# Token-major local attention and on-chip casts of the first two batches in a fused attention and MoE kernel

## The chip, the cores and the metric

The kernel runs on one core of a Trainium2 chip. The metric is the device time of one execution in microseconds (us). Before the change it is 374.99 us, the median of three runs (374.14 to 375.85).

A ratio is the mean time of one kernel's fast runs over the mean time of the other's fast runs of the same rounds, so it is not quite the ratio of the medians that are quoted beside it. The profile is of one execution, and its span is about 1.7 us shorter than the time of that execution.

## The reference

There are 8 batches, 8 heads of 64 columns, 512 local tokens and 32 global tokens per batch. Local queries see the keys at most 32 positions away and all global keys. Global queries see everything. A mixture-of-experts layer with a single expert (no routing) follows.

```
k_all, v_all = cat([k_g, k_l]), cat([v_g, v_l])
out_g = softmax(scale * q_g @ k_all.T) @ v_all
s_ll  = where(abs(pos_i - pos_j) <= 32, scale * q_l @ k_l.T, -1e9)
out_l = softmax(cat([scale * q_l @ k_g.T, s_ll])) @ v_all
x     = cat([out_g, out_l])            # (8 * 544) tokens x 512
h     = x @ w_in                       # 512 -> 2048
out   = (h * clip(h + 3, 0, 6) / 6) @ w_out
```

All inputs are fp32 in DRAM. The kernel computes in fp16, so every input is cast once.

## The kernel before

The work goes in 32 turns, one per pair of heads, four turns per batch. Turn p transposes the keys and queries of pair p + 2, computes the scores of pair p + 1 and the values of pair p, and fills the gaps with units of the previous batch's MoE (`M(n)` takes n units; one unit is four 512-column matmuls). A batch has 32 units.

```python
# loads: Pool's software queue casts fp32 to fp16 on the way in, one head at a time for batch 0
def load_head(b, h):
    qn, kn = nat[b]
    for t, src in ((kn, k_l), (qn, q_l)):
        nc.gpsimd.dma_start(out=t[:, :, h], in_=src[b, h].rearrange("(kb p) d -> p kb d", p=P))
# ... order at the start: k, q of batch 0, v of batch 0, then
load_qk(1, False); load_v(1)                 # batch 1
for m in range(NM): nc.gpsimd.dma_start(out=w_in_t[m], ...)     # 4 x 512 KB as fp16
for c4 in range(NC // 4): nc.gpsimd.dma_start(out=w_out_t[c4], ...)

# values: stationary = values, moving = exp of the scores; output is feature-major
nc.tensor.matmul(out=pav[:, 0:Sl], lhsT=vgz[:, b, h], rhs=EG[:, 0:Sl], ...)
for kb in range(NT):
    nc.tensor.matmul(out=pav[:, lo:lo + w], lhsT=vn[b % NV][:, kb, h], rhs=E[...], ...)
nc.scalar.activation(out=Ln, in_=pav[D:P, 0:Sl], func=LN)       # 1/sum = exp(-ln(sum))
nc.scalar.activation(out=Rc, in_=Ln, func=EXP, scale=-1.0)
nc.vector.tensor_tensor(out=xts[b][m][r], in0=Rc[r], in1=pavs[e][0:D, 0:Sl], op=mult)

for p in range(NPAIR):                       # cut to its order
    emit_T(p + 2); M(1); emit_QK(p + 1); M(2); emit_G(...); M(2); emit_AV(p, lambda: M(1)); M(2)
```

The softmax here doesn't subtract the row's maximum and nothing guards it: scores larger than these inputs give would overflow.

Of the kernel before, what the change touches and what calls it, by code (L numbers as in the profile page):

```python
# [14 lines left out]
def kernel(  # L15
# [12 lines left out]
    nc = tc.nc  # L28
# [6 lines left out]
    NQ = NM // 2  # L35
# [3 lines left out]
    WB = P + 2 * W  # L39
    HALF = 2 * WB - W  # L40
    EW = HALF + 2 * Sg
# [10 lines left out]

    WIN = []
    for kb in range(NT):
        lo = max(kb * P - W, 0)
        hi = min(kb * P + P + W, Sl)
        WIN.append((lo, hi - lo))
    COL = [0, WIN[0][1], 0, WIN[2][1]]
    assert WIN[0][1] + WIN[1][1] == HALF and WIN[2][1] + WIN[3][1] == HALF

    constp = ctx.enter_context(tc.tile_pool(name="constp", bufs=1))
    natp = ctx.enter_context(tc.tile_pool(name="natp", bufs=2))
    wrk = ctx.enter_context(tc.tile_pool(name="wrk", bufs=2))
    moew = ctx.enter_context(tc.tile_pool(name="moew", bufs=4))
# [6 lines left out]
    nc.scalar.preload_act_table_set("natural_log_exp_and_others")  # L71

    def const(name, shape, dtype=FP16):
        return constp.tile(shape, dtype, tag=name, name=name)

    ident = const("ident", [P, P])
    kgz = const("kgz", [P, B, NM, P])
    vgz = const("vgz", [P, B, H, P])
    qgT = const("qgT", [P, NM, B, Sg])
    half_col = const("half_col", [P, 1], FP32)  # L80
    mask = [const(f"mask{i}", [P, HALF]) for i in range(2)]
    NV = 3
    vn = [const(f"vn{i}", [P, NT, H, P]) for i in range(NV)]
    w_in_t = [const(f"win{m}", [P, dff]) for m in range(NM)]
    w_out_t = [const(f"wout{c}", [P, 4, dm]) for c in range(NC // 4)]

    nat = {}

    def load_qk(b, by_head):
        kn = natp.tile([P, NT, H, D], FP16, tag="kn", name="kn")  # L90
        qn = natp.tile([P, NT, H, D], FP16, tag="qn", name="qn")
        nat[b] = (qn, kn)
        if not by_head:
            for t, src in ((kn, k_l), (qn, q_l)):
                for kb in range(NT):
                    nc.gpsimd.dma_start(  # L96
                        out=t[:, kb],
                        in_=src[b, :, kb * P:(kb + 1) * P, :].rearrange("h s d -> s h d"))

    def load_head(b, h):  # L100
        qn, kn = nat[b]
        for t, src in ((kn, k_l), (qn, q_l)):
            nc.gpsimd.dma_start(out=t[:, :, h],  # L103
                                in_=src[b, h].rearrange("(kb p) d -> p kb d", p=P))

    def load_v_head(b, h):
        nc.gpsimd.dma_start(out=vn[b % NV][:, :, h, 0:D],  # L107
                            in_=v_l[b, h].rearrange("(kb p) d -> p kb d", p=P))

    def load_v(b):  # L110
        for kb in range(NT):
            nc.gpsimd.dma_start(  # L112
                out=vn[b % NV][:, kb, :, 0:D],
                in_=v_l[b, :, kb * P:(kb + 1) * P, :].rearrange("h s d -> s h d"))

    make_identity(nc, ident)
    load_qk(0, True)
    for h in range(4):
        load_head(0, h)

    gnat = []
    for src, nm in ((k_g, "kg"), (q_g, "qg")):
        t = const(nm + "n", [P, 2, H, D], FP32)
        for g in range(2):
            for b4 in range(4):
                nc.sync.dma_start(out=t[b4 * Sg:(b4 + 1) * Sg, g],
                                  in_=src[g * 4 + b4].rearrange("h s d -> s h d"))
        gnat.append(t)


    base = const("mbase", [P, WB])
    nc.vector.memset(base, 1.0)
    nc.gpsimd.affine_select(out=base, in_=base, compare_op=is_ge, fill=0.0,
                            base=0, pattern=[[1, WB]], channel_multiplier=-1)
    nc.gpsimd.affine_select(out=base, in_=base, compare_op=is_ge, fill=0.0,
                            base=2 * W, pattern=[[-1, WB]], channel_multiplier=1)
    nc.vector.tensor_copy(out=mask[0][:, 0:WB - W], in_=base[:, W:WB])
    nc.vector.tensor_copy(out=mask[0][:, WB - W:HALF], in_=base)
    nc.vector.tensor_copy(out=mask[1][:, 0:WB], in_=base)
    nc.vector.tensor_copy(out=mask[1][:, WB:HALF], in_=base[:, 0:WB - W])  # L140

    for h in range(2):
        load_v_head(0, h)
    load_head(0, 4)
    load_head(0, 5)

    nc.vector.memset(half_col, 0.5)
    for i in range(NV):
        nc.vector.memset(vn[i][:, :, :, D:P], 1.0)
    nc.vector.memset(kgz, 0.0)  # L150
    nc.vector.memset(vgz, 0.0)

    def pos(h):
        return (h % 2) * 2 + (h // 2) % 2

    for i in range(4):
        h0 = [h for h in range(4) if pos(h) == i][0]
        r = slice(i * Sg, (i + 1) * Sg)
        for qd in range(NQ):
            nc.vector.memset(vgz[r, :, 4 * qd + h0, D:P], 1.0)  # L160
            nc.gpsimd.dma_start(out=vgz[r, :, 4 * qd + h0, 0:D],  # L161
                                in_=v_g[:, 4 * qd + h0].rearrange("b s d -> s b d"))

    load_v_head(0, 2)
    load_v_head(0, 3)
    load_head(0, 6)
    load_head(0, 7)
    for h in range(4, 8):
        load_v_head(0, h)
    load_qk(1, False)  # L170
    load_v(1)
    for m in range(NM):
        nc.gpsimd.dma_start(out=w_in_t[m], in_=moe_w_in[m * P:(m + 1) * P, :])
    for c4 in range(NC // 4):
        nc.gpsimd.dma_start(
            out=w_out_t[c4],
            in_=moe_w_out[c4 * 4 * P:(c4 + 1) * 4 * P, :].rearrange("(c p) n -> p c n", p=P))


    gnat16 = []  # L180
    for t, nm in zip(gnat, ("kg", "qg")):
        t16 = const(nm + "n16", [P, 2, H * D])
        nc.vector.tensor_copy(out=t16, in_=t.rearrange("p g h d -> p g (h d)"))  # L183
        gnat16.append(t16)

    def emit_globals(g):
        psT = ps_tile("psGT", FP16)
        for w in range(2):
            for m in range(NM):
                nc.tensor.matmul(out=psT[:, (w * NM + m) * P:(w * NM + m + 1) * P],  # L190
                                 lhsT=gnat16[w][:, g, m * P:(m + 1) * P],
                                 rhs=ident, is_transpose=True)
        kv = psT.rearrange("p (w q pp b s) -> p w q pp b s", w=2, q=NQ, pp=2, b=4)
        for pp in range(2):
            for e in range(2):
                c0 = (e * 2 + pp) * Sg
                for qd in range(NQ):
                    nc.scalar.copy(
                        out=kgz[e * D:(e + 1) * D, g * 4:(g + 1) * 4, 2 * qd + pp, c0:c0 + Sg],
                        in_=kv[e * D:(e + 1) * D, 0, qd, pp])  # L200
        nc.vector.tensor_copy(
            out=qgT[:, :, g * 4:(g + 1) * 4],
            in_=psT[:, NM * P:2 * NM * P].rearrange("p (m b s) -> p m b s", m=NM, b=4))

    st = {}

    def emit_T(p):
        b, m = divmod(p, NM)
        qn, kn = nat[b]
        psT = ps_tile("psT", FP16)  # L210
        for w, t in enumerate((kn, qn)):
            for j in range(NT):
                nc.tensor.matmul(out=psT[:, w * Sl + j * P:w * Sl + (j + 1) * P],  # L213
                                 lhsT=t[:, j, 2 * m:2 * m + 2].rearrange("p h d -> p (h d)"),
                                 rhs=ident, is_transpose=True)
        kT = wrk.tile([P, Sl], FP16, tag="kT", name="kT", bufs=4)
        qT = wrk.tile([P, Sl], FP16, tag="qT", name="qT", bufs=4)
        nc.vector.tensor_copy(out=kT, in_=psT[:, 0:Sl])  # L218
        nc.scalar.copy(out=qT, in_=psT[:, Sl:2 * Sl])  # L219
        st[p] = dict(qT=qT, kT=kT)  # L220

    def emit_QK(p):
        b, m = divmod(p, NM)
        s = st[p]
        qT, kT = s["qT"], s["kT"]
        E = wrk.tile([P, 2, 2, EW], FP16, tag="E", name="E", bufs=3)
        s["E"] = E
        for half in range(2):
            pss = [ps_tile(f"psS{e}") for e in range(2)]
            for kb in (2 * half, 2 * half + 1):  # L230
                lo, w = WIN[kb]
                for e in range(2):
                    nc.tensor.matmul(out=pss[e][:, COL[kb]:COL[kb] + w],  # L233
                                     lhsT=kT[e * D:(e + 1) * D, kb * P:(kb + 1) * P],
                                     rhs=qT[e * D:(e + 1) * D, lo:lo + w])
                g0 = HALF + (kb % 2) * Sg
                for e in range(2):
                    nc.tensor.matmul(out=pss[e][:, g0:g0 + Sg],  # L238
                                     lhsT=kT[e * D:(e + 1) * D, kb * P:(kb + 1) * P],
                                     rhs=qgT[e * D:(e + 1) * D, m, b])  # L240
# [27 lines left out]
    def emit_AV(p, mid):  # L268
# [11 lines left out]
        for e in range(2):  # L280
# [18 lines left out]
            if e == 0:  # L299
                mid()  # L300
# [60 lines left out]
    for p in range(NPAIR):  # L361
# [4 lines left out]
        if p == 1:  # L366
            emit_globals(1)
# [52 lines left out]
```

## Time and profile before

These lines are from the page of the kernel before. They are the busy times, the rows of TensorE (PE), Pool, transfers (DMA) and moved data over 40 equal slices of 9.4 us, the two DMA queues that matter (packets, MB as written, share of 16 engines), and the chain of waits by engine.

```profile
PE 332.3 (89%) x2608; PEld 178.9 (48%) x2608; DVE 235.6 (63%) x489; ACT 239.5 (64%) x473; POOL 102.6 (27%) x132
...
PE   0078589999999999999999999999999999999995
...
POOL 8999436923240307003700343000000000000000
...
DMA  9999999999390469119961949100001000100202
GB/s 131 120 77 141 199 204 169 152 131 84 44 101 29 75 67 110 32 58 86 68 47 56 114 27 86 50 36 30 2 30 56 30 2 28 58 28 0 87 29 56
...
q0 software_dynamic: 104896, 17.05, 60.7%
q1 hardware_dynamic: 9344, 9.97, 7.9%
...
PE 62%; DVE 12%; POOL 9%; ACT 9%; issue 3%; DMA 3%; POOLq 0%
```

From the sixth slice on TensorE is busy at eight tenths or more. Until then it is not, and in that time the transfers are at nine tenths or more: for the first ten slices, to 94 us, their row has no gap. The chain of waits in order of time shows what the start hangs on. Columns are start, length, and what ran.

```profile
1.34 0.89 POOL kn L103
...
20.32 0.97 POOL kn L96
...
31.99 3.49 POOL vn_82 L112 x4
35.48 0.55 POOL win_84 L173
...
36.44 11.94 DMA win_86<-in_moe_w_in_dram
48.43 0.61 PE psH L324
```

Pool issues the casting loads one after the other until 36 us, and the first MoE matmuls then wait for `w_in`. I read off two points from the timeline of TensorE: the transposes that open a turn (`psT<-ident,kn`), and the first MoE matmul (`psH`), which stands right behind the opening of turn 4, the first turn of batch 1.

### The profile page before, as it was taken

How to read it: one execution, taken by the hardware profiler on the slowest of the kernel's cores; microseconds unless marked ns; L12 is line 12 of the kernel's file. 1: busy time of each engine (PE TensorE's matmuls, PEld its weight loads, DVE VectorE, ACT ScalarE, POOL GpSimd, SP SyncE). 2: the span in 40 equal slices, each digit the busy share in tenths (PEclk: the TensorE clock that was granted, in tenths of full speed). 3: DMA queues.
4: the chain of work that ended last, by engine and by line, in shares of the span. 5: the costliest groups of instructions: out<-in, count | busy, mean ns of one | idle time of the engine just before them, and what ended most of it. 6: DMA issues, size and time to landing. Idle time of an engine off the chain costs nothing.

```text
span 375.0 us, 6707 instructions
## 1 busy us (share of the span) xinstructions
PE 332.3 (89%) x2608; PEld 178.9 (48%) x2608; DVE 235.6 (63%) x489; ACT 239.5 (64%) x473; POOL 102.6 (27%) x132
## 2 busy tenths in 40 slices
PE   0078589999999999999999999999999999999995
PEld 0046335555455554554555445545555445544472
DVE  7855667645875487548764587448754885296171
ACT  1059969745984599547965698458945895375070
POOL 8999436923240307003700343000000000000000
PEclk9998969999999999999999999999999999999999
DMA  9999999999390469119961949100001000100202
GB/s 131 120 77 141 199 204 169 152 131 84 44 101 29 75 67 110 32 58 86 68 47 56 114 27 86 50 36 30 2 30 56 30 2 28 58 28 0 87 29 56
DMA packets 114272, 27.44 MB, mean 73 GB/s; under 512 B 107328, under 2 KB 109376, under 8 KB 114240
## 3 DMA queue, kind: packets, MB, share of 16 engines
q0 software_dynamic: 104896, 17.05, 60.7%
q1 hardware_dynamic: 9344, 9.97, 7.9%
q8 instruction: 20, 0.33, 0.4%
q14 instruction: 12, 0.10, 0.1%
HBM read 35.13 MB, written 8.91 MB: 117 GB/s over the span
## 4 chain that ended last, share of the span: by engine, by line
PE 62%; DVE 12%; POOL 9%; ACT 9%; issue 3%; DMA 3%; POOLq 0%
PE po L338 27%; PE psH L324 23%; PE pav L292 4%; ACT Rc L301 3%; DMA win_86<-in_moe_w_in_dram 3%; ACT Ln L298 3%; PE pav L284 2%; POOL kn L103 2%; POOL qn L103 2%; PE psGA L256 2%; POOL vn_81 L107 1%; POOL vgz L161 1%; PE pg L295 1%; POOL kn L96 1%; POOL qn L96 1%
## 5 line engine op out<-in xcount | busy, mean ns | idle before, releaser
L298 ACT ACTIVATE Ln<-pav 64x512 f32<-64x512 f32 x64 | 37.9, 593 | 45.4 <-PE pav L292 38.1
L342 DVE COPY ot<-po 128x512 f32<-128x512 f32 x34 | 23.5, 692 | 25.6 <-PE po L338 25.2
L96 POOL DMA_DIRECT2D kn<-in_k_l_dram x28 | 24.7, 898 | 44.3 <-PE psT L213 36.5
L219 ACT COPY qT<-psT 128x512 f16<-128x512 f16 x32 | 18.8, 586 | 22.9 <-DVE kT L218 22.7
L96 POOL DMA_DIRECT2D qn<-in_q_l_dram x28 | 24.8, 926 | 6.7 <-PE psH L324 1.9
L284 PE MATMUL pav<-EG,vgz 128*128 128x512 f16 x64 | 24.7, 386 | 1.4 <-ACT qT L219 1.1
L244 DVE TENSOR_TENSOR E<-E,mask_79 128x352 f16<-128x352 f16 x64 | 19.8, 337 | 8.4 <-ACT E L242 8.2
L244 DVE TENSOR_TENSOR E<-E,mask_80 128x352 f16<-128x352 f16 x64 | 20.9, 340 | 5.4 <-ACT E L242 3.4
L324 PEld LDWEIGHTS <-win_86 128*128 128x128 f16 x144 | 14.2, 98 | 18.4 <-DMA win_86<-in_moe_w_in_dram 2.4
L324 PEld LDWEIGHTS <-win_87 128*128 128x128 f16 x144 | 14.1, 98 | 15.9 <-DMA win_87<-in_moe_w_in_dram 0.5
L301 ACT ACTIVATE Rc<-Ln 128x512 f32<-128x512 f32 x32 | 20.0, 626 | 0.7
L233 PEld LDWEIGHTS <-kT 64*128 64x128 f16 x256 | 13.6, 95 | 13.6 <-issue 13.1
L324 PEld LDWEIGHTS <-win_85 128*128 128x128 f16 x144 | 14.1, 98 | 11.0 <-issue 2.1
L112 POOL DMA_DIRECT2D vn_82<-in_v_l_dram x12 | 10.6, 918 | 31.4 <-PE pg L295 31.4
L190 PE MATMUL psGT<-ident,kgn_192 128*128 128x128 f16 x8 | 1.2, 304 | 20.1 <-DVE kgn_192 L183 20.1
L324 PEld LDWEIGHTS <-win_84 128*128 128x128 f16 x144 | 14.1, 98 | 9.8 <-issue 0.6
L238 PEld LDWEIGHTS <-kT 64*128 64x128 f16 x256 | 12.8, 94 | 6.7 <-issue 6.6
L218 DVE COPY kT<-psT 128x512 f16<-128x512 f16 x32 | 13.4, 418 | 2.9 <-PE psT L213 2.9
L286 PE MATMUL pg<-EG,vgz 128*128 128x32 f16 x64 | 10.8, 180 | 4.7 <-DVE xg_199 L314 4.7
L213 PE MATMUL psT<-ident,qn 128*128 128x128 f16 x128 | 12.9, 225 | 0.0
L112 POOL DMA_DIRECT2D vn_81<-in_v_l_dram x8 | 7.1, 909 | 21.1 <-PE pg L295 20.6
L213 PE MATMUL psT<-ident,kn 128*128 128x128 f16 x128 | 12.8, 225 | 0.0
(1097 smaller groups left out, 1112.3 us busy)
## 6 DMA issues: line engine op xcount, KB each, us to landing
out_dram<-ot SPq DMA_DIRECT2D x32, 256.0 KB, 2.0
kn<-in_k_l_dram POOLq DMA_DIRECT2D x28, 128.0 KB, 4.1
qn<-in_q_l_dram POOLq DMA_DIRECT2D x28, 128.0 KB, 5.3
vn_82<-in_v_l_dram POOLq DMA_DIRECT2D x12, 128.0 KB, 3.9
vn_83<-in_v_l_dram POOLq DMA_DIRECT2D x8, 128.0 KB, 5.1
vn_81<-in_v_l_dram POOLq DMA_DIRECT2D x8, 128.0 KB, 4.8
kgn<-in_k_g_dram SPq DMA_DIRECT2D x8, 64.0 KB, 2.7
kn<-in_k_l_dram POOLq DMA_DIRECT2D x8, 64.0 KB, 3.5
```

The lines of the kernel that those rows point to most:

```text
L96: nc.gpsimd.dma_start(out=t[:, kb], in_=src[b, :, kb * P:(kb + 1) * P, :].rearrange("h s d -> s h d"))
L103: nc.gpsimd.dma_start(out=t[:, :, h], in_=src[b, h].rearrange("(kb p) d -> p kb d", p=P))
L112: nc.gpsimd.dma_start(out=vn[b % NV][:, kb, :, 0:D], in_=v_l[b, :, kb * P:(kb + 1) * P, :].rearrange("h s d -> s h d"))
L213: nc.tensor.matmul(out=psT[:, w * Sl + j * P:w * Sl + (j + 1) * P], lhsT=t[:, j, 2 * m:2 * m + 2].rearrange("p h d -> p (h d)"), rhs=ident ...
L219: nc.scalar.copy(out=qT, in_=psT[:, Sl:2 * Sl])
L244: nc.vector.tensor_tensor(out=E[:, e, half, 0:HALF], in0=E[:, e, half, 0:HALF], in1=mask[half], op=mult)
L284: nc.tensor.matmul(out=pav[:, 0:Sl], lhsT=vgz[:, b, h], rhs=EG[:, 0:Sl], start=True, stop=False, skip_group_check=True)
L298: nc.scalar.activation(out=Ln[e * D:(e + 1) * D], in_=pav[D:P, 0:Sl], func=LN)
L301: nc.scalar.activation(out=Rc, in_=Ln, func=EXP, scale=-1.0)
L324: nc.tensor.matmul(out=ps[:, 0:n], lhsT=w_in_t[m][:, c * P:(c + 1) * P], rhs=rhs(m), start=(m == 0), stop=(m == NM - 1))
L338: nc.tensor.matmul(out=po[t][:, 0:dm], lhsT=gts[c][:, t * P:(t + 1) * P], rhs=w_out_t[c // 4][:, c % 4], start=(c == 0), stop=(c == NC - 1))
L342: nc.vector.tensor_copy(out=ot, in_=po[t][:, 0:dm])
```

## The change

The intent is twofold. The attention becomes token-major: for tiles of 128 queries, the exp of the scores is the stationary operand and the values, with a column of ones, are the 65 moving columns. The sum of a query is then one element per partition, a short VectorE reciprocal replaces Ln and Exp on ScalarE, and the result is transposed back on TensorE. The start also changes: batches 0 and 1 are loaded in fp32 by the hardware queues and cast by VectorE, ScalarE and Pool, so that Pool no longer issues these loads.

```diff
+    def load_stage(p, engs):
+        for i, src in enumerate((k_l, q_l, v_l)):
+            t = wrk.tile([P, 2, NT, D], FP32, tag="stg", name="stg", bufs=NSTG)        # NSTG = 11
+            engs[i].dma_start(out=t.rearrange("p h kb d -> p (h kb) d"), in_=src[b, 2*m:2*m+2]...)
+    def cast_stage(p, engs):
+        for eng, o, i in zip(engs, dst, st[p]["fs"]):
+            (nc.scalar.copy if eng == "act" else getattr(nc, eng).tensor_copy)(out=o, in_=i)
+    def vshift(b, hs):      # the second half tile of values starts 64 partitions later
+        nc.vector.tensor_copy(out=vbs[b % NV][0:D, :, hs, 0:D], in_=vts[b % NV][D:P, :, hs, 0:D])
+    def vglob(b):           # global values beside it
+        for u in range(NT):
+            nc.sync.dma_start(out=vbs[b % NV][r, u, :, 0:D], in_=vg[r, b])
+        nc.sync.dma_start(out=vgs[b % NV][r, :, 0:D], in_=vg[r, b])
... values, token-major
+                    nc.tensor.matmul(out=o, lhsT=E[:, 0, e, w*P:(w+1)*P], rhs=vt[:, w, h, 0:D+1], ...)
+                    nc.tensor.matmul(out=o, lhsT=E[:, 1, e, w*P:(w+1)*P], rhs=vb[:, (w-1)%NT, h, 0:D+1], ...)
+            nc.vector.reciprocal(out=rc, in_=pv[:, :, :, D:D + 1])
+            nc.vector.tensor_tensor(out=xn[...], in0=pv[:, :, :, 0:D], in1=rc.to_broadcast(...), op=mult)
... and back
+            nc.tensor.matmul(out=psX[:, w*P:(w+1)*P], lhsT=xn[:, w], rhs=ident, is_transpose=True)
... the order
+    load_stage(0..3); w_in (Pool); load_stage(4..7, all on SP); w_out (Pool)
     for p in range(NPAIR):
+        if b == 0: cast_stage(p + NM, ("vector", "gpsimd", "gpsimd"))
+        if m == NM - 1: vshift(b + 1, all heads); vglob(b + 1)
         emit_T(p + 2); M(1); emit_S(p + 1, 0); M(2); emit_S(p + 1, 1); emit_SG(p + 1); M(2); emit_AV(p)
+        M(3 if b != 1 else 1)
+        emit_X(p)
```

Value buffers go from three sets to two, and batch 1's turns take two MoE units fewer each, so eight units are left for the end.

## The prediction

> **What bounds the kernel now.** TensorE (PE), after a slow start. The page gives PE 89% busy, ACT 64%, DVE 63%; the chain of waits is 62% PE. The chain in order of time shows a steady period of 40.2 us per batch (92.76, 132.97, 173.19 us are the same point of successive batches). Of it the MoE's 128 matmuls of 512 columns take 128 x 0.2156 = 27.6 us (starts in the timeline), so attention has about 12.6 us, 3.15 us per head pair. From the timeline I add up, per pair: transposes 0.45, scores 0.42 of work plus about 0.2 entering and leaving the half-array matmuls and 0.4 to 0.6 waiting for PSUM, global queries 0.25, values 2 x 0.63.
> The start: DVE fills constants until 19 us, so the first matmul comes at 20.1 us; Pool issues casting DMAs one by one (about 0.74 us each) until 41 us; the first MoE matmul waits for w_in until about 48.4 us. From there 7 x 40.2 + 45 us of tail make the 375.
>
> **What the change does.**
> - Values: two 512-column and eight 160/192-column matmuls per pair become sixteen of 65 columns, each with its own weight load. The trace has five successive 32-column matmuls with new weights in 0.12 us, 25 ns each; the Trainium skill, "TensorE: Matmul & The Clock Gate", section "Wait — 56ns, not 53.3ns?", states the same 25 ns floor. I estimate 16 x 30 ns = 0.47 us, global part 10 x 25 ns = 0.25, transposing back 4 x 56 = 0.22. Total about 0.95 instead of 1.26 us.
> - Scores: sixteen 128-column matmuls, in pairs on array halves: about 0.45 us, as before, but in two pieces, so twice the entry cost. Global scores 5 x 29 = 0.15 instead of 0.25.
> - Pair sum: about 2.35 us against 2.6 before, without PSUM waits. Those should shrink: score tiles are now asked for in twos, and the value tile is freed by DVE reciprocal and multiply instead of Ln, Exp and multiply.
> - ACT loses Ln (64 x 593 ns) and the exp of it (32 x 626) but its score exps widen from 416 to 512 columns and it takes half of the output copies. DVE loses the 64-partition multiplies (682 ns each), gains wider masks and 128x256 multiplies, about as much. Both stay under PE.
> - I expect a period of 38.1 us, 2.1 less per batch.
> - Start: hardware-queue loads, casts on three engines, less filling on DVE, w_in issued after the first casts. First score matmul near 16 us, batch 0's attention done near 30 to 33 us instead of MoE starting at 48. Worth 15 to 18 us, the largest part; loads of batch 1 and w_out may take some of it back. Eight MoE units move from batch 1 to the end, neutral for PE.
>
> **Time.** 33 (batch 0) + 32 (batch 1 with 24 MoE units) + 6 x 38.1 + 53 (40 units, the global MoE 14, end 4.6) = 347 us; range 337 to 359. Faster by over 2%: 0.96; within: 0.03; slower: 0.01.
>
> **What would show it.** The same MoE point in successive batches 38 us apart; value matmuls starting 30 ns apart; first psH matmul at 30 to 35 us; page parts 1: DVE and ACT shares rising above 68%, PE's share over 90%; tail of MoE-only work about 53 us.
>
> **What would make it wrong.** Fp32 loads in 256-byte pieces running slower than the casting ones, so that batch 1 or w_out hold up PE until 60 to 70 us (355 us or more); a DVE so full that its evictions stall PE in the stage with two MoE evictions per unit; weight loads of 128x128 scores not hidden behind 65 columns (then period 39 to 40).

## More of the kernel before

```profile
44.23 0.39 PE L213 MATMUL psT<-ident,kn 128*128 128x128 f16 x4
44.45 0.39 PE L213 MATMUL psT<-ident,qn 128*128 128x128 f16 x4
44.68 0.38 PE L324 MATMUL psH<-xt_324,win_84 128*128 128x512 f16 x1
```

So turn 4 opens at 44.2 us. (The texts written before the runs call this "the fifth pair starts".) It needs the keys and queries of batch 1's third pair, because a turn transposes two pairs ahead. TensorE's queue is in order here, so the MoE of batch 0 cannot start before these loads have landed.

## The result, and the profile after

The changed kernel takes 388.62 us, the median of four runs (387.87 to 392.24). The ratio to before is 1.037, with an interval of 1.032 to 1.042: it is slower, where 347 us was predicted.

These are the same lines of the page after.

```profile
PE 330.5 (85%) x3024; PEld 178.9 (46%) x3024; DVE 235.0 (61%) x593; ACT 213.0 (55%) x450; POOL 89.5 (23%) x115
...
PE   0118348769989999999899999999999999999995
...
POOL 4607264660306030703070307030000000000000
...
DMA  7999999990579049904892399049000100110202
GB/s 129 167 222 214 195 195 175 124 126 2 63 122 108 3 50 104 133 5 54 82 142 15 49 106 133 6 53 107 24 1 30 70 13 2 56 54 0 83 28 54
...
q0 software_dynamic: 79744, 13.90, 47.3%
q1 hardware_dynamic: 38976, 16.00, 20.0%
...
PE 33%; DMA 24%; issue 22%; POOL 9%; DVE 8%; ACT 2%; ACTq 0%; SPq 0%; DVEq 0%; POOLq 0%
```

Pool is relieved, as intended (its first slices fall from 8999 to 4607). TensorE's row nevertheless fills later, and its share of the chain falls from 62% to 33%. The data moved in the third to sixth slice rise from 77 to 204 GB/s before to 195 to 222 GB/s. The opening of turn 4 and the first MoE matmul are 19 us later than before:

```profile
63.01 0.63 PE L167 MATMUL psT<-ident,kn 128*128 128x128 f16 x4
63.43 0.63 PE L167 MATMUL psT<-ident,qn 128*128 128x128 f16 x4
63.86 1.49 PE L281 MATMUL psH<-xt,win 128*128 128x512 f16 x3
```

I divide both spans at the openings of turns 4, 9 and 29. Turns 9 to 29 are twenty turns, or five batches, of steady running.

| stretch | before, us | after, us | difference |
|---|---|---|---|
| 0 to turn 4 | 44.2 | 63.0 | +18.8 |
| turn 4 to 9 (batch 1 and one turn) | 55.5 | 51.7 | -3.8 |
| turn 9 to 29 (five batches) | 201.1 | 193.3 | -7.8 |
| turn 29 to the end | 74.2 | 79.3 | +5.1 |
| span | 375.0 | 387.3 | +12.3 |

Of the -3.8 and the +5.1, about 6.9 us are only moved: the eight units that go from batch 1 to the end (8 x 4 x 0.2156 us). Without that move batch 1 would be some 3 us longer than before and the end some 2 us shorter. The token-major attention gains where it was meant to gain. The start loses more than that gain. The chain in order of time names the staged loads:

```profile
10.92 15.07 DMA stg<-in_k_l_dram
...
28.14 5.86 DMA stg<-in_v_l_dram
34.00 16.66 DMA stg<-in_k_l_dram
...
50.69 0.43 DVE kn L108
...
51.61 0.40 DVE xn L241
...
52.06 0.39 PE psX L257 x2
...
56.71 11.09 DMA stg<-in_q_l_dram
```

At 51 us one sees a second thing: TensorE waits for `xn`, an attention result of batch 0, and `xn` stands in VectorE's queue behind the cast of a key tile of batch 1 that has only just landed. The waits of the whole span (total, times, longest) show how much of this there is:

```profile
DVE kn L108 <- DMA stg<-in_k_l_dram: 29.7, 7, 15.6
DVE vb L123 <- DMA vt<-in_v_l_dram: 28.1, 6, 6.1
...
PE psX L257 <- DVE xn L241: 19.4, 17, 9.7
PE psT L167 <- DVE kn L108: 15.0, 1, 15.0
```

The second line is another copy at the head of VectorE's queue: the shift of the next batch's values by 64 partitions, which waits up to 6.1 us for their load, in almost every batch. The Trainium skill, "TensorE: Matmul & The Clock Gate", section "Architectural detail: the array is 16× 32×32, not 1× 128×128", says that the queues of ScalarE and VectorE are strictly first in, first out. This trace agrees: VectorE stood 15.6 us at one cast.

Three causes could thus be at work at the start: the staged loads load the transfer engines more than the casting ones did; the casts and copies at the heads of in-order queues hold up work that is ready; or the order of the loads is wrong. In the steady part the shift is a suspect.

### The profile page after: what moved, and what is told of

It is laid out like the page before. It is cut to its first block, busy times and chain, and to the rows that moved or that the text cites. A ratio compares the mean times of both kernels' runs of the same rounds, so it can differ in the third digit from the quotient of the medians.

```text
span 387.3 us, 7678 instructions
## 1 busy us (share of the span) xinstructions
PE 330.5 (85%) x3024; PEld 178.9 (46%) x3024; DVE 235.0 (61%) x593; ACT 213.0 (55%) x450; POOL 89.5 (23%) x115
## 3 DMA queue, kind: packets, MB, share of 16 engines
HBM read 35.13 MB, written 8.91 MB: 114 GB/s over the span
## 4 chain that ended last, share of the span: by engine, by line
PE 33%; DMA 24%; issue 22%; POOL 9%; DVE 8%; ACT 2%; ACTq 0%; SPq 0%; DVEq 0%; POOLq 0%
PE po L295 14%; PE psH L281 13%; DMA stg<-in_k_l_dram 8%; DMA vt<-in_v_l_dram 8%; POOL qn L118 4%; POOL kn L118 3%; DMA stg<-in_q_l_dram 3%; DVE E L195 2%; DVE gt L286 2%; PE psT L167 2%; POOL vt L118 2%; DVE xn L241 2%; DMA stg<-in_v_l_dram 2%; DMA kgf<-in_k_g_dram 1%; PE psS L190 1%
## 5 line engine op out<-in xcount | busy, mean ns | idle before, releaser
L295 PE MATMUL po<-wout,gt 128*128 128x512 f16 x544 | 126.5, 379 | 0.0
L281 PE MATMUL psH<-xt,win 128*128 128x512 f16 x512 | 122.7, 383 | 0.0
L286 DVE SCALAR_TENSOR_TENSOR gt<-t,psH 128x512 f16<-128x512 f32 (+1 forms) x144 | 90.7, 653 | 31.9 <-ACT t L284 30.8
L284 ACT ACTIVATE t<-psH,half_col 128x512 f32<-128x512 f32 (+1 forms) x144 | 92.0, 669 | 20.3 <-PE psH L281 18.2
L193 ACT ACTIVATE E<-psS 128x512 f16<-128x512 f32 x128 | 70.3, 617 | 9.8 <-PE psS L190 9.4
L281 PEld LDWEIGHTS <-win 128*128 128x128 f16 x576 | 52.7, 98 | 49.4 <-issue 1.2
L295 PEld LDWEIGHTS <-gt 128*128 128x128 f16 x544 | 49.8, 98 | 53.0
L195 DVE TENSOR_TENSOR E<-E,mk 128x512 f16<-128x512 f16 x128 | 51.4, 425 | 17.0 <-ACT E L193 15.4
L190 PE MATMUL psS<-qT,kT 64*128 64x128 f16 x512 | 28.3, 235 | 2.0 <-ACT qT L176 2.0
L241 DVE TENSOR_TENSOR xn<-pav,rc 128x256 f16<-128x256 f32 x64 | 26.2, 421 | 1.2
## 6 DMA issues: line engine op xcount, KB each, us to landing
stg<-in_v_l_dram SPq DMA_DIRECT2D x8, 256.0 KB, 10.5
```

Of the source, the lines that this page charges most:

```text
L190: nc.tensor.matmul(out=pss[e][:, w * P:(w + 1) * P], lhsT=kT[r, c0:c0 + P], rhs=qT[r, w * P:(w + 1) * P])
L193: nc.scalar.activation(out=E[:, ch, e], in_=pss[e], func=EXP, scale=qk_scale)
L195: nc.vector.tensor_tensor(out=E[:, ch, e], in0=E[:, ch, e], in1=mk[:, ch].rearrange("p w c -> p (w c)"), op=mult)
L241: nc.vector.tensor_tensor(out=xn[:, 2 * w2:2 * w2 + 2].rearrange("p w (e d) -> p w e d", e=2), in0=pv[:, :, :, 0:D], in1=rc.to_broadcast([ ...
L281: nc.tensor.matmul(out=ps[:, 0:n], lhsT=w_in_t[m][:, c * P:(c + 1) * P], rhs=rhs(m), start=(m == 0), stop=(m == NM - 1))
L284: nc.scalar.activation(out=t1[:, 0:n], in_=ps[:, 0:n], func=RELU, bias=half_col, scale=1.0 / 6.0)
```

## The experiments

Every run has the outputs of the reference, except two that are wrong. "Before" was run beside each; its medians lay between 375.2 and 376.0 us. The openings of the turns of the main runs are collected here, in us. The line of the kernel named e12 is that of its first run.

| kernel | time, median | turn 4 opens | 4 to 9 | 9 to 29 | 29 to end |
|---|---|---|---|---|---|
| before | 374.99 | 44.2 | 55.5 | 201.1 | 74.2 |
| after | 388.62 | 63.0 | 51.7 | 193.3 | 79.3 |
| e2 before, staged | 396.54 | 66.5 | 53.8 | 201.1 | 74.2 |
| e1 after, casting loads | 372.79 | 41.6 | 56.0 | 195.0 | 82.0 |
| e13 after, half of each staged load | 371.30 | 49.9 | 49.0 | 191.4 | 79.3 |
| e10 after, shift by a transfer | 386.39 | 63.1 | 52.3 | 188.0 | 79.3 |
| e11 e1 and shift by a transfer | 366.53 | 42.0 | 55.7 | 188.0 | 79.3 |
| e14 e11 and 3.1 MB unread | 379.53 | 52.0 | 57.5 | 188.0 | 79.6 |
| e17 the same in 1 KB pieces | 372.42 | 47.2 | 55.2 | 188.0 | 79.9 |
| e12 | 363.24 | 49.8 | 44.2 | 188.0 | 79.3 |
| e16 e12, units back in batch 1 | 361.48 | 49.9 | 49.2 | 188.0 | 72.5 |

### Casting loads put back: e1 and e1b

```diff
-    load_stage(0..3, ...); cast_stage(0..3, ...); load_stage(4..7, ...); cast_stage(p + NM, ...)
+    for h in range(4): ld(0, h, "kq")        # Pool's casting loads by head, in the order of before
+    ...; load_cast(1, "qk"); load_cast(1, "v"); w_in; w_out
```

The constant fills that Pool did in the changed kernel go back to VectorE with it. The run e1b is the same with `w_in` ahead of batch 1.

> The changed kernel with the loads of the first two batches undone: casting DMAs from the Pool queue, in the order of the kernel before (batch 0 by head, batch 1, then w_in, w_out); attention and the rest as changed. Theory L (all of the loss lies in the staged fp32 loads of batches 0 and 1; the attention change itself gains about 1.9 us a batch): first MoE matmul (psH) back near 45 to 50 us instead of 63.9, batch 1 done near 85 instead of 104.4, total 362 to 370 us, faster than before. Rival A (the new attention pipeline is slow in the first two batches whoever loads them: longer chains through DVE and ACT): psH start stays at 60 us or later, or batch 1 still takes 40 us, total 380 us or more.

> As e1_soft, but w_in is issued before the loads of batch 1. If what lets MoE start is the order of issue on one Pool queue, psH starts near 36 to 40 us and the total falls by a further 5 to 10 us (355 to 362); if batch 1's data then holds up the PE, no gain over e1_soft.

Measured: e1 takes 372.79 us (371.31 to 376.30), ratio 0.993 (0.987 to 0.999). It has 16 us of the loss back, though less than I had expected, and turn 4 opens at 41.6 us. Its profiled execution had a mean granted clock of 0.92 and is the slowest of the four, so its last two stretches read too long. e1b takes 374.30 us, ratio 0.996 (0.991 to 1.000). With `w_in` first, turn 4 opens at 50.6 us and not earlier: it needs batch 1's keys and queries, which had moved behind `w_in`. The start is a question of what has to be loaded before turn 4, not only of when the weights come.

### The kernel before, with staged loads: e2

```diff
# in the kernel before
+    load_stage / cast_stage as in the changed kernel, seven staging buffers
-    load_head(0, h) ...; load_v_head(0, h) ...; load_qk(1, False); load_v(1)
+    cast_stage(0..3, ("vector", "act", "gpsimd")); load_stage(4..7, all SP); cast_stage(p + NM, ...)
-    t1, ot: 4 buffers
+    t1: 3 buffers, ot: 2 buffers                  # for space
```

With Pool's queue thus empty, `w_in` and `w_out` are issued earlier than in before.

> The kernel before, with its own compute, but batches 0 and 1 loaded in fp32 through the hardware queues and cast on chip, in the way of the changed kernel. Theory L (these staged loads alone are the loss at the start): the fifth pair starts 10 to 19 us later than before's 44.2, and the whole is 386 to 400 us. Rival C (the loss comes from the changed compute order, and the staged loads cost nothing): 372 to 378 us.

Measured: 396.54 us (395.15 to 398.65), ratio 1.057 (1.052 to 1.061). The timeline of TensorE:

```profile
66.49 0.39 PE L224 MATMUL psT<-ident,kn 128*128 128x128 f16 x4
66.72 0.39 PE L224 MATMUL psT<-ident,qn 128*128 128x128 f16 x4
66.94 0.81 PE L335 MATMUL psH<-xt,win 128*128 128x512 f16 x3
```

Turn 4 opens 22 us later than in before, more than the 10 to 19 expected, and the last two stretches are unchanged at 201.1 and 74.2 us, so the smaller buffers cost nothing there. The staged loads, with the earlier weights that go with them, cost the loss with none of the token-major attention. Theory L holds and rival C falls.

### Less to load, or another order: e4, e9

e4 loads no MoE weights at all (the result is wrong). e9 holds both weights back behind the values of batch 0 and of batch 1.

```diff
# e4
-    for m in range(NM): nc.gpsimd.dma_start(out=w_in_t[m], ...)     # and w_out
+    nc.gpsimd.memset(w_in_t[0], 0.01)                               # one tile for all
# e9: a copy into each weight tile makes its load wait
+    nc.gpsimd.tensor_copy(out=w_in_t[m][:, 0:2], in_=vts[0][:, 0, 6, 0:2])
+    nc.gpsimd.tensor_copy(out=t[:, 0, 0:2], in_=vts[1][:, 0, 2, 0:2])       # w_out, in turn 1
```

> The changed kernel with no weight loads at all: one w_in and one w_out tile are filled with a constant and used for all (result wrong on purpose; race free). Theory C (the staged loads are slow because w_in and w_out, issued at 9.7 and 32 us, share the 16 DMA engines with them): the second pair's k, issued near 11 us, lands within 6 us instead of 15, the batch 1 loads issued near 34 us land within 8 us instead of 16.7, psH starts at 40 us or earlier, total 355 us or less. Rival P (256-byte fp32 pieces through the hardware queue[...] are slow by themselves): k still takes over 10 us, psH starts after 50 us, total over 372.

> The changed kernel with the weight loads held back by a data dependence: w_in until batch 0's last values are cast, w_out until batch 1's second pair is cast. Theory C (weights issued first take the DMA engines from the staged loads): the second pair's k lands near 16 us as in e4_noweights instead of 26, first score matmul near 22 us instead of 29.9. MoE then starts at 45 to 55 us instead of 63.9, total 372 to 380. Rival T (it is the total amount that has to pass before MoE can go on, order does not matter): batch 0 comes earlier, but MoE starts within 3 us of 63.9 and the total stays 384 to 390.

Measured: e4, in one look (its state is unknown), takes 369.92 us, and turn 4 opens at 44.7 us, 18.3 us earlier than in after. That lies between what theory C (355 us or less) and rival P (over 372 us) expected. e9 takes 388.8 to 392.1 us in three runs, ratio 1.038 (1.033 to 1.043). Its fourth run took 577.7 us at a granted clock of 0.57 and was the profiled one, so I read nothing from its profile, and whether batch 0 came earlier is not known. Taking 4.2 MB out of the start is worth 18 us; holding the same 4.2 MB back for a while is worth nothing (the copies that hold them back also take places in Pool's queue). So the amount that has to be moved counts more than this order.

### Which wait at a queue's head: e5, e8

e5 issues the copies of the global values of batches 0 and 1 from Pool, because they stood on the SP queue ahead of staged loads. e8 moves batch 1's key casts from VectorE to Pool.

```diff
# e5
+        eng = nc.gpsimd if b < 2 else nc.sync
# e8
-            cast_stage(p + NM, ("vector", "gpsimd", "gpsimd"))
+            cast_stage(p + NM, ("gpsimd", "gpsimd", "gpsimd"))
```

> The changed kernel with the small copies of v_g into the value tiles of batches 0 and 1 issued from the Pool queue instead of the SP queue, where they stand before the second pair's loads and hold them until 10.9 us. Theory O (order on the SP queue): second pair's k issued near 2 us, lands near 10 to 12 us instead of 26, first score matmul near 14 instead of 29.9, psH up to 10 us earlier, total 377 to 382. Theory C or P (the DMA engines are full anyway): the first pairs come earlier but the last loads of batch 1 do not, total within 3 us of 387.

> The changed kernel with batch 1's k casts on Pool instead of DVE. In the changed kernel DVE stood from 42 to 50.7 us at the cast of a k tile that had not landed, and the multiplies behind it held the PE for 9.7 us. Theory Q (a cast in an in-order compute queue turns a late load into a stop of everything behind it): the 9.7 us wait goes, the transposes of 52.2 us come near 43 us; but the PE's own queue has the next pair's transposes two places on, and they need the same late tile, so the first MoE matmul moves by at most 1 to 5 us and the total is 382 to 387. If the cast's place in DVE's queue is the whole cause, MoE starts near 54 us and the total is 376 to 380.

Measured: e5 takes 384.82 us (383.17 to 388.17), ratio 1.025 (1.018 to 1.031). The second pair's keys are transposed by 11.9 in place of 27.1 us and the first scores come at 14.8 in place of 29.9 us, but turn 4 opens at 58.6, only 4.4 us earlier, and the whole is inside what theory C or P expected. e8 takes 390.98 us, ratio 1.042 (1.038 to 1.046): its fifth transposes come at 41.1 in place of 52.2 us, so the wait at VectorE's cast is gone, and turn 4 still opens only at 57.8 us, and nothing is gained in all (382 to 387 us had been expected). With the waits at queue heads taken away, others come up a few us later, as one expects when the loads themselves are late.

### Bytes or casts: e13, e14

e13 is the changed kernel with each staged load cut to one head of the pair; the cast writes it to both heads, so every load, cast and queue position stays (wrong). e14 is the version with casting loads and the shift by a transfer (e11, below), and adds twelve fp32 loads of 256 KB that nothing reads and no cast.

```diff
# e13
-            t = wrk.tile([P, 2, NT, D], FP32, tag="stg", ...);  in_=src[b, 2 * m:2 * m + 2]
+            t = wrk.tile([P, 1, NT, D], FP32, tag="stg", ...);  in_=src[b, 2 * m:2 * m + 1]
-            (... tensor_copy)(out=o, in_=i)
+            (... tensor_copy)(out=o, in_=i.to_broadcast([P, NT, 2, D]))
# e14, after the global values of batch 0
+    for i in range(12):
+        t = wrk.tile([P, 2, NT, D], FP32, tag="stg", name="stg", bufs=NSTG)
+        nc.sync.dma_start(out=..., in_=(k_l, q_l, v_l)[i % 3][7, ...])      # 256-byte pieces
```

> The changed kernel, but each staged load brings one head of the pair (128 KB of fp32 in place of 256 KB), and the cast writes it to both heads: every load, cast and queue position stays, the staged bytes fall from 6.3 to 3.1 MB (wrong result on purpose). Theory B (bytes at the transfer engines, about 200 GB/s): the fifth pair starts at 44 to 51 us instead of 63.0, and the whole is 368 to 378 us. Rival C (the casts and their in-order queues): fifth pair at 57 us or later, whole 382 to 390 us.

> The kernel of e11 with twelve plain fp32 loads of 256 KB (3.1 MB, as much as staging adds) that nothing reads, issued on the same hardware queue after batch 0's global values. Theory B: the start loses 10 to 16 us, the whole is 376 to 383 us. Rival C: no cast was added, so at most 4 us, 365 to 371 us.

Measured: e13 takes 371.30 us (370.03 to 371.97), ratio 0.988 (0.985 to 0.991), with turn 4 at 49.9 us. e14 takes 379.53 us (378.78 to 380.30), ratio 1.011 (1.009 to 1.013), 13 us more than e11, with turn 4 at 52.0 us (e11: 42.0). Both are inside what theory B expected. Taking load off the transfers gives the loss back with every cast in place; putting load on brings it back with no cast added. The casts and their in-order queues are where the wait shows, not what causes most of it. Both runs change the bytes and the number of pieces together; the next one divides these. Two limits remain. Staging itself changes neither the number of pieces nor what is read from DRAM (35.13 MB on both pages), only the bytes written on chip, so e13 and e14 show that load on the transfers costs time at the start, and only e1 and e2 show what staging costs. And in e14 the copies of batch 1's global values stand on the SP queue behind the added loads (issued from 50.2 us, in e11 from 23.9), and TensorE's first values of batch 1 wait for them until 70.5 us (e11: 58.7, for the shift). Part of what e14 loses after turn 4 can be this order; the 10.0 us at turn 4 come before these copies are needed.

### Bytes or pieces: e17

A staged load moves rows of 64 values. On chip that is a piece of 256 bytes in fp32; a casting load writes the same row as 128 bytes. e17 is e14 with pieces of 1 KB.

```diff
-        [...].rearrange("h (kb p) d -> p (h kb) d", p=P)
+        [...].rearrange("h (p r) d -> p h (r d)", p=P)
```

> e14 with its twelve unread loads (3.1 MB) in pieces of 1 KB in place of 256 bytes. Theory Y (the bytes cost): 376 to 382 us, as e14 (379.5). Theory Z (the pieces cost, each about the same whatever its length up to 1 KB): the start loses a quarter of what e14 lost against e11, 2 to 5 us, and the whole is 368 to 372 us. In between, both count.

Measured: 372.42 us (372.02 to 372.64), ratio 0.990 (0.985 to 0.995). Against e11 that is 5.9 us for the same bytes that cost 13.0 us in e14. It lies just outside what "the pieces" expected and far from what "the bytes" expected, so both count, and the pieces count more. At turn 4 it is 5.2 us (47.2 us) against e14's 10.0. From e14 a 256-byte piece costs 13.0 us / 12,288 = 1.06 ns, and from e17 a 1 KB piece 5.9 us / 3,072 = 1.9 ns: four times the length for about 1.8 times the cost.

The traces give the pace of the loads themselves. The transfers of before between 30 and 36 us are casting loads but for one packet; those of after between 25 and 31 us are staged loads alone. In both windows the row of the transfers is full.

```profile
DMA packets 6871, 0.88 MB, mean 147 GB/s; under 512 B 6870, under 2 KB 6870, under 8 KB 6870
```

```profile
DMA packets 5189, 1.31 MB, mean 218 GB/s; under 512 B 5189, under 2 KB 5189, under 8 KB 5189
```

A casting piece took 6 us / 6871 = 0.87 ns, a staged one 6 us / 5189 = 1.16 ns. The first is an upper bound: in this window Pool issued four loads of 1,024 pieces each in 3.49 us (the chain of before), 0.85 ns per piece, so the casting loads went at Pool's pace, and the transfer engines may have had room. The 24,576 staged pieces of batches 0 and 1 (2 batches x 3 tensors x 512 rows x 8 heads) then cost about 24,576 x 0.28 ns = 7 us more than casting pieces, an estimate from these two windows. That is a third to less than a half of the 16 to 21 us that e1 and e2 show. The rest (a casting piece cheaper than 0.87 ns, the order in which whole pairs come, the wait for a staging buffer, the cast after the landing) I did not separate.

### VectorE's queue: e6, e7, e10, e11

In the steady part, a batch of after shows this chain in order of time:

```profile
104.43 6.23 DMA vt<-in_v_l_dram
...
110.78 0.69 DVE vb L123
111.50 0.76 DVE E L195 x2
112.26 0.60 DVE ot L299
...
113.53 0.43 DVE xn L241
...
114.01 0.28 PE psX L257 x2
```

The shift of the next batch's values waits 6.2 us for its load at the head of VectorE's queue, and `xn`, which TensorE needs, comes out behind it. The load is late because there are only two sets of value buffers: it cannot be issued before the last value matmul of the batch that frees its set. My first remedy was a third set (e6, on e1). e7 is e6 with batch 0 in twelve loads of 128 KB and `w_in` ahead of batch 1.

```diff
# e6
-    NV = 2
+    NV = 3                                   # staging buffers 11 -> 3
# e7, in addition
+    load_cast(0, "qk"); load_cast(0, "v"); ...; w_in; load_cast(1, ...)
```

> e1_soft with three sets of value tiles instead of two (the room comes from the staging buffers, which that kernel hardly uses). Theory V (a second loss: with two sets, the casting load of batch b+2's values can only be issued when batch b's last value matmul is done; it lands some 6 us later, and the shifting copy that waits for it already stands in DVE's queue before masks and evictions, so DVE stops 3 to 4 us per batch): DVE's waits for the value loads (28.1 us in all in the changed kernel) vanish, the time between the same transposes of successive batches falls from 38.7 to 37.6 us, and the total is 6 to 10 us below e1_soft, 362 to 367. If V is wrong the total stays within 2 us of e1_soft's 372.8.

> e6_soft_nv3 with batch 0 loaded in twelve casting DMAs of 128 KB (all heads of 128 tokens) instead of 24 of 64 KB, and w_in issued before batch 1's loads. If the start is bound by the number of DMAs that Pool has to issue (0.74 to 0.88 us each whatever their size), all of batch 0 has been issued at 12 us, its attention is done near 28 us, batch 1's loads are issued by 26 us, the first MoE matmul comes near 32 us instead of 42, and the total falls to 350 to 357. If it is bound by the DMA engines, it falls by less than 4 us against e6_soft_nv3.

Measured: e6 takes 378.24 us (377.06 to 380.43), ratio 1.008 (1.003 to 1.012); e7 takes 376.12 us, ratio 1.003 (0.997 to 1.009). e6 misses what was expected. e7 is 2.1 us below e6, which fits "bound by the DMA engines", but it moves `w_in` too, so it does not settle what Pool's issue costs. In e6 VectorE still waits at the shift: 19.0 us in four waits between 90 and 310 us, against 24.3 us in five in e1. Its loss against e1 lies at the start: turn 4 opens at 51.1 in place of 41.6 us, and before it VectorE waits up to 8.5 us at a shift and TensorE up to 7.6 us for the `xn` behind it. I read this so, that with a third set the schedule places the shift earlier in VectorE's queue, where it waits much as before; the runs show the waits, not the reason. A buffer more does not help by itself when the waiting copy stands in the queue of an engine that has other work. So e10 and e11 take the copy out of that queue: the shift of a whole batch becomes one transfer within on-chip memory.

```diff
-        nc.vector.tensor_copy(out=vbs[b % NV][0:D, :, hs, 0:D], in_=vts[b % NV][D:P, :, hs, 0:D])
+        if hs == slice(0, H):
+            nc.sync.dma_start(out=vbs[b % NV][0:D, ...], in_=vts[b % NV][D:P, ...])
+        else: ... as before                  # the parts of batch 0
```

> The changed kernel, but the shift of a whole batch's values by 64 partitions (batches 1 to 7) is done by one transfer inside the on-chip memory instead of a VectorE copy that stands in VectorE's queue behind the load of those values. Theory D (VectorE's queue held by that copy: 28 us of waiting in the changed kernel, 6 times): the steady stretch from the 9th to the 29th pair shrinks from 193.3 us to 180 to 188, the whole to 376 to 384 us. Rival N (that wait is hidden: PE has enough queued work): within 2 us of 388.6, and the stretch stays at 191 to 194.

> The kernel of e1 (batches 0 and 1 by casting loads, in before's order) with the same shift by a transfer. Theory D: the fifth pair still starts near 41.6 us, batch 1 shortens from 56 us towards 50, and the whole falls from 372.8 to 360 to 368 us. Rival N: 371 to 375 us, with batch 1 unchanged at 55 to 57 us.

Measured: e10, the changed kernel with this alone, takes 386.39 us (384.39 to 387.71), ratio 1.029 (1.024 to 1.033). The whole falls by only 2 us (the two profiled spans differ by 4.6), which theory D did not expect; the steady stretch falls from 193.3 to 188.0 us, at the edge of the 180 to 188 that it did expect. The waits between 90 and 310 us show where most of the stretch's gain comes from; the first two lines are of after, the last is of e10.

```profile
DVE vb L123 <- DMA vt<-in_v_l_dram: 25.1, 5, 6.1
...
PE psX L257 <- DVE xn L241: 5.5, 11, 1.6
```

```profile
PE psX L261 <- DVE xn L245: 1.1, 3, 0.7
```

Of the 25.1 us that VectorE waited, only 5.5 reached TensorE. In e10 1.1 us of that is left, so 4.4 of the 5.3 us that the stretch gained are this wait. Idle time of an engine off the critical path counts only as far as it reaches the one that is on it. e11, on e1, takes 366.53 us (365.95 to 366.74), ratio 0.976 (0.973 to 0.978), 6 us less than e1 and inside what theory D expected, but for another reason in part: batch 1 did not shorten (55.7 against 56.0 us), against D. There TensorE now waits 5.7 us once for the transfer itself, which took 18.9 us to land while the row of the transfers was full.

### Versions that beat both: e12, its second run, and e16

e12 is e7 with the shift by a transfer and the global values of batch 0 loaded first. The run named e15_m3 was e12 a second time on another chip. e16 is e12 with the eight MoE units back in batch 1.

```diff
# e12, on e7
+    nc.gpsimd.dma_start(out=vg[r, 0], ...)   # ahead of batch 0's loads, not behind them
+    (the shift as in e10)
# e16, on e12
-        M(3 if b != 1 else 1)
+        M(3)
```

> The attempt at a version that beats both: casting loads for batches 0 and 1, the global values of batch 0 first, the first MoE weights before batch 1, three sets of value buffers, and the shift by a transfer. Theory D: 355 to 366 us, batch 1 at 45 to 50 us and no wait of VectorE for value loads over 2 us. Rival N: 371 to 377 us, as the same without the transfer shift (376.1).

> A second look at e12 as it is, on another chip: 361 to 365 us by one look if its time is stable; the waits of TensorE in batch 1 for the normalized values and for the shifted values stay at 4.4 and 1.4 us at longest.

> e12 with three MoE units, as in every other batch, instead of one between the value matmuls and the transposes of batch 1's pairs. Theory F (the deferral only moves work that TensorE has to do anyway): batch 1 lengthens by 4 to 7 us, the part after the last attention pair shortens by 5 to 7 us, the whole stays within 2 us of 363.2. Rival G (the deferral exposes the chain from the values to the transposes in batch 1): the whole falls by 3 us or more, to 357 to 360 us. Rival H (the units in batch 1 wait for their weights): it rises by 3 us or more.

Measured: e12 takes 363.24 us (363.03 to 364.24), ratio 0.968 (0.965 to 0.971), and 363.19 us in the second look (one run, state unknown). Its stretch from turn 4 to 9 is the shortest of all (44.2 us), but turn 4 opens at 49.8 us, 7.8 us later than in e11; at turn 9 it is 3.7 us ahead of e11 (94.0 against 97.7 us). e16 takes 361.48 us (361.24 to 361.66), ratio 0.960 (0.956 to 0.965), the fastest. Its stretch from turn 4 to 9 is 5.1 us longer and its end 6.8 us shorter than e12's. That is theory F: the deferral moves work that TensorE has to do anyway. It costs 1.7 us between the two spans, which are from different chips; that part of these units fills waits which batch 1 has in any case fits this, but was not tested by itself. e12 changes two things against e7, so its 13 us over e7 are not divided between them.

## Why the prediction was wrong

The mechanism of the steady part was right; the start was wrong by its sign. For the steady part I add up the time from one group of matmuls to the next between turns 9 and 29, per pair: values with their global part and the transposing back go from 1.29 to 1.09 us (0.95 had been predicted), scores from 1.01 to 0.67, global queries from 0.24 to 0.16 (0.15 predicted). The four terms of the predicted sum, and what the profile of after measures (turn 8 opens at 102.6 us, the attention ends at 334.3 us):

| term | predicted, us | measured, us | error |
|---|---|---|---|
| batch 0, to the start of the MoE | 33 | 63.0 | +30.0 |
| batch 1 with 24 MoE units | 32 | 39.6 | +7.6 |
| six batches | 6 x 38.1 = 228.6 | 231.7 (38.6 each) | +3.1 |
| tail | 53 | 53.0 | 0 |

- **The step that failed** is, as the prediction put it, "Start: hardware-queue loads, casts on three engines, less filling on DVE, w_in issued after the first casts. First score matmul near 16 us, batch 0's attention done near 30 to 33 us instead of MoE starting at 48. Worth 15 to 18 us, the largest part". The first score matmul came at 29.9 us and the MoE at 63.9 us. The step took Pool's issue time as the limit of the start, since the chain named Pool. Pool was indeed relieved, but the transfers then became the limit: the change gave them dearer pieces, 1.16 in place of at most 0.87 ns each, and a staged load took a median of 8.9 to 10.5 us from issue to landing (before's casting loads of 64 and 128 KB as written: 3.1 to 5.3). e2 shows the sign with the old attention (+22 us at turn 4), e13 and e14 that the load on the transfers is the cause. How the loss divides between the pieces and the rest stays open. The Trainium skill, "Trainium Kernel Development and Optimization", section "Key Constraints", says that transfers from the SP, ScalarE and Pool queues run on the same 16 engines, and that issuing from several saves only issue time. This agrees: with the loads on the queues of SP and ScalarE Pool's row fell and turn 4 still opened 18.8 us later, and in e14 loads that nothing reads, issued from SP, made those issued from Pool land later (batch 0's value loads a median of 6.4 us from issue to landing, 3.7 in e11; 13 us in all). The page of before gave a warning, transfers in flight without a gap for 94 us, but no proof that they were at their limit. What Pool's relief alone would have been worth no run separates.
- **A second slip in the same step**: turn 4 needs keys and queries of batch 1, and TensorE takes its queue in order. "Batch 0's attention done" therefore had to wait for loads of batch 1, which I had counted only as something that "may take some of it back". e1b shows the dependence: `w_in` ahead of batch 1's loads delayed turn 4 by 9 us.
- **Batch 1** was 7.6 us longer than predicted. Loads were still arriving (the transfers' row is full until about 87 us). It was shortest in e12 (34.4 us), with casting loads, the first weights ahead of batch 1 and the shift out of VectorE's queue; which of these does it was not separated.
- **The period** of 38.1 us was 38.6. The part of it that I had not foreseen is the shift at the head of VectorE's queue; without it, it is 188.0 / 5 = 37.6 us, better than predicted. Before is 40.2.
- **The value matmuls** start 30 to 31 ns apart (16 of them in 0.49 us), where 30 had been predicted. The Trainium skill, "TensorE: Matmul & The Clock Gate", section "Wait — 56ns, not 53.3ns?", gives N / 2.4 GHz + 2.5 ns for warm matmuls of N columns, so 29.6 ns for 65, an estimate from that page; this trace agrees:

```profile
199.84 0.19 PE L232 MATMUL pav<-vt,E 128*128 128x65 f16 x1
199.87 0.19 PE L235 MATMUL pav<-vb,E 128*128 128x65 f16 x1
199.90 0.19 PE L232 MATMUL pav<-vt,E 128*128 128x65 f16 x1
```

- **The eight units at the end**, "neutral for PE", were nearly so: 1.7 us (e16 against e12).
- **VectorE and ScalarE above 68%** did not come: 61% and 55%, since the span grew and ScalarE's busy time fell by 26.5 us.
- What would make it wrong was named first, "Fp32 loads in 256-byte pieces running slower than the casting ones", with 60 to 70 us for TensorE's hold-up. That is what happened, and it had been given next to no chance (0.01 for slower). The trace of before held part of what was needed to weigh it, the bytes of the loads before the MoE and the full row of the transfers; what a staged piece costs it does not show.

## What to carry to other kernels

When a chain of waits names the engine that issues loads, look at the row of the transfers under it before you free that engine: if it has no gap, a faster issue may buy nothing, and a form of load with dearer pieces can be a loss. The row alone does not decide it; a run with half the load, as e13, or with loads that nothing reads, as e14, does. An operation that waits for a load should not stand in the in-order queue of an engine that others depend on; more buffers need not help, since a schedule may only move the wait, and a transfer can do the copy. Undo a change in parts before you discard it: the new attention, with the shift done by a transfer, is worth 13 us over five batches (201.1 to 188.0 us), and with casting loads, a better order of them, and the shift out of VectorE's queue the whole is 4% faster than before.

## What the Trainium skill lacked or had wrong

- "DMA: Bandwidth & Descriptors" says that casts in a transfer must be issued from Pool, but not what they cost the transfer engines beside a plain load. Here, in windows with a full row, a casting piece (128 bytes written) took at most 0.87 ns and a plain fp32 piece (256 bytes) 1.16 ns: casting on the way in was the cheaper one.
- "DMA: Bandwidth & Descriptors", section "Why small descriptors are slow (HBM only)", counts 11 cycles for a 256-byte descriptor, 27% of it overhead, and names descriptor metadata as a second cost, without a time for it. By the cycles alone a kilobyte costs 4 x (8 + 3) = 44 cycles in 256-byte pieces and 32 + 3 = 35 in one piece, so the same bytes should cost 80% in 1 KB pieces, an estimate from that page. The runs show 5.9 against 13.0 us, 45% (5.2 against 10.0 us at turn 4). These are differences of whole kernels, so the figure holds for this start and not for the engines alone, and it shows only that the cycles by themselves do not account for it.
- The same section says that transfers within on-chip memory do not suffer from small pieces. The 256 KB shift in 128-byte pieces took a median of 4.7 us from issue to landing in the steady part and 18.9 us at the start, when the row of the transfers was full. No run here isolates the pieces' share of that, so the sentence is neither confirmed nor contradicted.
